# Moving the loads of q, k, v (pairs 4 to 10) and of expert 0's weights to other steps of a sorted-attention and mixture kernel

## The chip, the core and the metric

One core of a Trainium2 chip runs the whole program. A core has TensorE (PE, with its weight loads listed as PEld), VectorE (DVE), ScalarE (ACT), GpSimd (POOL), SyncE (SP) and 16 DMA engines, which all transfers share. The metric is the time of the program on the device in microseconds (us); lower is better.

## The reference

```python
for _ in range(5):                      # P: 8x8 per (batch, head)
    P = exp(P - max(P)); P /= sum(P, -1); P /= sum(P, -2)
k_sorted = einsum('bhij,bhjcd->bhicd', P, k_blocks)      # 8 blocks of 96 rows
v_sorted = einsum('bhij,bhjcd->bhicd', P, v_blocks)
scores = (q_b @ k_sorted_b.T) / 8; attn = softmax(scores)
x = (attn @ v_sorted_b) -> [3072, 512]                   # 4 batches x 768, 8 heads x 64
G = exp(x @ w_gate - max); 8 rounds: G /= rows; G /= columns; G *= 3072/8
out = sum over 8 experts e of G[:, e] * (relu(x @ w1[e]) @ w2[e])
```

The inputs are float32: q, k, v of 4 x 8 x 768 x 64, w1 of 8 x 512 x 1024, w2 of 8 x 1024 x 512.

## The kernel before, in words

The work has three parts. First, five rounds of normalisation on the 8 x 8 matrices of all 32 heads (DVE and ACT, lines 136 to 147), while the first loads run. Second, attention head by head, in 34 steps of a loop written out by hand (line 388). Third, the experts 1 to 7, which are long rows of matrix products (lines 505 to 531). Expert 0 needs x of a whole batch only, so its products are cut into pieces (`l1_piece` with w1, `l2_piece` with w2) and put between the products of the attention steps from step 9 on; `fill()` hands them out, four times a step.

Heads go in pairs: pair n holds the heads 2n and 2n + 1, and there are 16 pairs. The life of a pair is this:

- `load_pair(n)` (line 65) issues three transfers on POOL's queue, k, v and q, of 192 KB each as stored (they are cast from float32 on the way). They go to the buffers `kvr` and `qr`, of which there are six, so pair n takes the buffer of pair n - 6.
- `relayout(n)` (line 75; at step 2n - 4) is a copy on POOL from `kvr` into `kv` (two buffers). POOL works in order, so it holds up what stands behind it until k and v have landed and until the sort of pair n - 2 has read the buffer. For pair 0 ACT does it in parts.
- `build_R` (line 286) makes the sorting weights R of two heads on POOL, at each even step s for the heads s + 4 and s + 5.
- `sort_kv(g)` (line 296; at step g - 2) does six products on PE with kv and R (line 302). ACT copies their result to `kvT` (line 305; three buffers, head g takes buffer g modulo 3), and SP issues a DMA transpose of its half with v into `v1` (line 308).
- `q_transpose(n)` (line 253; at step 2n - 2) has six transposes on PE and the copies to `qT`.
- `scores(g)` (lines 317 to 324; step g), `weights(g)` (the exponential, line 328), `a_transpose(g)` (PE line 339 and an ACT copy, line 341, a step later), `attend(g)` (line 346, with `v1`), `normalise(g)`, and `x_transpose(n)` (PE line 364, ACT line 367). The heads 16 to 29 are transposed by DMA instead (line 332).

So a step's ACT work up to step 9 is the copy of line 305, the exponential, the copy of line 341, and in turn two copies of q or one of x.

The order is the program's own: `manual_schedule` keeps every engine's instructions as they are written. Each engine works in that order and waits by semaphores. Which step issues a pair's load stands in a table, `loads` (lines 385 and 386); pairs 0 to 4 are loaded ahead of everything (lines 88 to 92), pair 5 behind the first relayout (line 375), then pair 6 at step 1, 7 at 3, 8 at 5, 9 at 7, 10 at 9, 11 at 10, 12 at 11, 13 at 13, 14 at 15 and 15 at 17. `load_expert(0)` issues w1 and w2 of expert 0 (1024 KB each as stored) at the end of step 2. w1 is first used behind the gate's products at step 10, w2 at step 12.

Of the kernel before, what the change touches and what calls it, by code (L numbers as in the profile page):

```python
# [12 lines left out]
BF16 = mybir.dt.bfloat16  # L13
# [11 lines left out]
def kernel(  # L25
# [11 lines left out]
    nc = tc.nc  # L37
# [4 lines left out]
    N, Dm, E, F = 3072, 512, 8, 1024  # L42
# [22 lines left out]
    def load_pair(n):  # L65
        kv = rawp.tile([128, 2, 2, CL, D], BF16, name="kvr")
        qr = rawp.tile([128, 2, CL, D], BF16, name="qr")
        for t, r in ((k, kv[:, 0]), (v, kv[:, 1]), (q, qr)):
            nc.gpsimd.dma_start(
                out=r.rearrange("p h c d -> p h (c d)"),  # L70
                in_=bass.AP(tensor=t.tensor, offset=t.offset + 2 * n * S * D,
                            ap=[[CL * D, 128], [S * D, 2], [1, CL * D]]))
        raw_t[n] = (kv, qr)

    def relayout(n):

        kv = iop.tile([128, 2 * CL, 2, D], BF16, name="kv")
        nc.gpsimd.tensor_copy(kv.rearrange("p c t d -> p t c d"),  # L78
                              raw_t[n][0].rearrange("p t h c d -> p t (h c) d"))
        kv_t[n] = kv  # L80
# [8 lines left out]
    load_pair(1)  # L89
    load_pair(2)  # L90
    load_pair(3)
    load_pair(4)


    P9 = pp.tile([32, 9, 9], F32)
# [65 lines left out]
    wp = ctx.enter_context(tc.tile_pool(name="wp", bufs=2))  # L161
    wg = ones.tile([128, 4, E], BF16)
    w1t, w2t = [], []

    def load_expert(e):
        w1e = wp.tile([128, 4, F], BF16, name="w1e")
        w2e = wp.tile([128, 8, Dm], BF16, name="w2e")
        nc.gpsimd.dma_start(out=w1e, in_=moe_w1[e].rearrange("(kk k) f -> k kk f", k=128))  # L168
        nc.gpsimd.dma_start(out=w2e, in_=moe_w2[e].rearrange("(fb k) f -> k fb f", k=128))
        w1t.append(w1e)  # L170
        w2t.append(w2e)

    xtp = ctx.enter_context(tc.tile_pool(name="xtp", bufs=1))
    xtT = xtp.tile([128, 4, N], BF16)
# [45 lines left out]
    def batch_pieces(b):  # L220

        out_ = []
        for c in (2 * b, 2 * b + 1):
            out_ += [(0.65, l1_piece(c, fb)) for fb in range(8)]

            out_ += [(1.72, l2_piece(c, tt, nc.scalar.copy if c >= 2 and tt in (1,)
                                     else nc.vector.tensor_copy)) for tt in range(3)]
        return out_
# [9 lines left out]
    def fill():  # L238
        if slots[0] > 0:
            ahead[0] += sum(c for c, _ in pieces) / slots[0]  # L240
            slots[0] -= 1
        while pieces and ahead[0] >= pieces[0][0] / 2:
            c, run = pieces.pop(0)
            run()
            ahead[0] -= c
# [7 lines left out]
    def q_transpose(n):  # L253


        qr = raw_t[n][1]
        tq = psF.tile([128, 2, CL // 2, 128], BF16, name="psF")
        for e in range(2):
            for c in range(CL // 2):
                nc.tensor.matmul(tq[:, e, c], qr[:, e, 2 * c:2 * c + 2].rearrange("p l d -> p (l d)"),  # L260
                                 Ibf, is_transpose=True, start=True, stop=True)
        for e in range(2):
            to = qT_[0:64, n % 2, e, 0:S].rearrange(
                "p (i c l h) -> p l c i h", i=NB, l=2, h=CH)
            for l in range(2):
                (nc.vector.tensor_copy if e == 0 and n > 1 else nc.scalar.copy)(  # L266
                    to[:, l], tq[64 * l:64 * l + 64, e].rearrange("p c (i h) -> p c i h", h=CH))
# [18 lines left out]
    def build_R(eng, src, g0, n):  # L286
        eng.tensor_tensor(
            out=R[:, g0:g0 + n],
            in0=mkap(src, [src.ap[0], [1, n], [32, 8], [0, CH]], off=g0),
            in1=mkap(mask16, [mask16.ap[0], [0, n], [0, 8], [1, CH]]),  # L290
            op=ALU.mult)
# [4 lines left out]
    def sort_kv(g):  # L296

        kv, e = kv_t[g // 2], g % 2
        kvps = psB.tile([128, 2, 512], F32, name="psB")
        kvf = mkap(kvps, [kvps.ap[0], [1, CL * 128]])  # L300
        for cl in range(CL):
            nc.tensor.matmul(kvf[:, cl * 128:(cl + 1) * 128],  # L302
                             kv[:, e * CL + cl].rearrange("p t d -> p (t d)"),
                             R[:, g].rearrange("p i c -> p (i c)"), start=True, stop=True)
        nc.scalar.copy(kvT_[:, g % NKT, :, 0:96].rearrange("p i (l c) -> p i l c", c=CH),  # L305
                       mkap(kvps, [kvps.ap[0], [CH, NB], [128, CL], [1, CH]]))

        nc.sync.dma_start_transpose(
            out=v1_[:, g % NVB, :, 0:64],
            in_=kvT_[64:128, g % NKT].rearrange("p i c -> p (i c)"))  # L310

    def scores(g):

        qT, kvT = qT_[:, (g // 2) % 2, g % 2], kvT_[:, g % NKT]
        sps = psB.tile([128, 2, 512], F32, name="psB")
        for i in range(NB):
            nc.tensor.matmul(sps[:, i // 4, (i % 4) * 96:(i % 4 + 1) * 96],  # L317
                             qT[:, i * BL:i * BL + 128], kvT[:, i, 0:96],
                             start=True, stop=True)
        s4 = sps[0:96, :, 0:384].rearrange("p a (i c) -> p a i c", c=96)  # L320
        mx = sp.tile([96, 2, 4], F32, name="mx")
        nc.vector.reduce_max(out=mx, in_=s4, axis=AX.X)  # L322
        ssb = sp.tile([96, 2, 4, 96], F32, name="ssb")
        nc.vector.tensor_sub(ssb, s4, mkap(mx, [mx.ap[0], [4, 2], [1, 4], [0, 96]]))  # L324
        ssb_t[g] = ssb

    def weights(g):
        nc.scalar.activation(out=at_[:, g % NAT, :, 0:96],  # L328
                             in_=ssb_t.pop(g).rearrange("p a i c -> p (a i) c"),
                             func=AF.Exp, scale=scale)  # L330
        if g in DT:
            nc.sync.dma_start_transpose(
                out=aT_[:, g % NTT, 0:S].rearrange("p (i c) -> p i c", c=BL),
                in_=at_[:, g % NAT].rearrange("p i c -> p (i c)"))

    def a_transpose(g):
        ta = psF.tile([128, NB, 96], BF16, name="psF")
        for i in range(NB):
            nc.tensor.matmul(ta[:, i, :], at_[:, g % NAT, i], Ibf[0:96, 0:96],  # L339
                             is_transpose=True, start=True, stop=True)  # L340
        nc.scalar.copy(aT_[0:97, g % NTT, 0:S], ta[0:97].rearrange("p i c -> p (i c)"))
# [30 lines left out]
    sort_kv(0)  # L372
    build_R(nc.gpsimd, Pb, 2, 2)
    relayout(1)
    load_pair(5)
    nc.gpsimd.dma_start(out=wg, in_=moe_w_gate.rearrange("(kk k) e -> k kk e", k=128))
    NP = NH // 2
    step = {g: g + (2 if g in DT else 1) for g in range(NH)}
# [3 lines left out]
    x_step = {}  # L382
    for n in range(NP):
        x_step.setdefault(max(step[2 * n], step[2 * n + 1]) + 1, []).append(n)
    loads = {2 * n - 11: n for n in range(6, 11)}
    loads.update({10: 11, 11: 12, 13: 13, 15: 14, 17: 15})
    new = []
    for s in range(NH + 2):
        if s % 2 == 0 and s + 4 < NH:
            build_R(nc.gpsimd, Pb, s + 4, 2)  # L390
        if s < NH:
            scores(s)
        if s == 0:
            sort_kv(1)
            onesc = ones.tile([128, 128], F32)
            nc.gpsimd.memset(onesc, 1.0)
            nc.gpsimd.memset(glog[:, NT, :], EPS / 128)
            nc.gpsimd.memset(glog[:, 0:NT, E:E + 1], EPS)
        fill()
        if 0 <= s - 1 < NH and s - 1 not in DT:  # L400
            a_transpose(s - 1)
        fill()
        if s + 2 < NH:
            sort_kv(s + 2)
        if s < NH:
            weights(s)
        if s % 2 == 0:
            if 0 < s and s // 2 + 1 < NP:
                q_transpose(s // 2 + 1)
            if s // 2 + 2 < NP:  # L410
                relayout(s // 2 + 2)
        for n in x_step.get(s, []):
            x_transpose(n)
            if n % 4 == 3 and n < NP - 1:
                new = [(0.7, gate_piece(n // 4))] + batch_pieces(n // 4)
        fill()
        for g in at_step.get(s, []):
            attend(g)
            normalise(g)
        if s in loads:  # L420
            load_pair(loads[s])
        fill()
        if new:
            add(new, {9:34,17:40,26:28}[s])
            new = []
        if s == 2:
            load_expert(0)
        if s == 31:

            late_ = pp.tile([1, 8], BF16)  # L430
            nc.gpsimd.tensor_copy(late_, at_[0:1, 31 % NAT, 0, 0:8])
            load_expert(1)
# [57 lines left out]
    for it in range(8):  # L490
# [8 lines left out]
            out=gl, in0=gl, scalar=float(N) / E,  # L499
# [5 lines left out]
    for e in range(1, E):  # L505
        if e + 1 < E:
            load_expert(e + 1)
        for nc4 in range(6):
            for fb in range(AHEAD if (e, nc4) == (1, 0) else 0, 8):
                l1_tile(e, nc4, fb)  # L510
            for tt in range(4):
# [8 lines left out]
                for c0 in range(0, Dm, W):  # L520
                    oacc = psF.tile([128, Dm], F32, name="psF")
                    for fb in range(8):
# [3 lines left out]
                        out=osbl[:, t, c0:c0 + W], in0=oacc[:, 0:W],  # L526
                        scalar=glog[:, t, e:e + 1], in1=osbl[:, t, c0:c0 + W],
                        op0=ALU.mult, op1=ALU.add)
                    if e == E - 1:
                        nc.sync.dma_start(out=out[t * 128:(t + 1) * 128, c0:c0 + W],  # L530
                                          in_=osbl[:, t, c0:c0 + W])
# [30 lines left out]
```

## Time and profile before

| what | value |
|---|---|
| median of 3 runs | 761.83 us (761.48 to 763.7) |
| the profiled execution | 760.26 us, its span 758.5 us |
| mean granted TensorE clock | 0.993 |
| DMA queue of POOL (software) | 26.23 MB, 22.8% of 16 engines' span |
| DMA queue of SP (hardware) | 13.25 MB, 8.4% |
| read from HBM, written | 52.45 MB, 6.29 MB |

The profile's page gives each engine's busy time, then the span in 40 slices of 19 us with one digit of busy tenths per engine. A row of the timeline gives the start, the duration, the engine, the line, what is written and read, how often, and in brackets how long the engine sat idle before and what ended that. A row of the windows view gives the window, its length, the busy time and number of instructions of PE, PEld, DVE, ACT and POOL, the granted TensorE clock (1.00 is full speed), the share of the DMA engines and the GB/s moved. A row of the DMA view ends with the time from the issue of a transfer to its landing.

### The profile page before, as it was taken

The page shows a single profiled execution, that of the slowest core. Times are in us where ns is not written, and L with a number is a line of the kernel's source. Part 1 is how long each engine was busy: PE and PEld are TensorE (multiplying, and loading weights), DVE is VectorE, ACT ScalarE, POOL GpSimd, SP SyncE. Part 2 cuts the span into 40 slices and gives each one's busy share as a digit, 9 for nine tenths or more (in the row PEclk, how much of TensorE's full clock was granted, in tenths as well). Part 3 has the DMA queues.
Part 4 walks back from the last instruction along what each step waited for, and adds up shares of the span by engine and source line. Part 5 has one row for each costly group of instructions (what it writes and reads, how often), then busy time and mean ns, then how long its engine had stood idle before and what let it go on. Part 6 is the DMA issues. An engine that isn't in the chain of part 4 may idle for free.

```text
span 758.5 us, 10311 instructions
## 1 busy us (share of the span) xinstructions
PE 725.8 (96%) x4274; PEld 367.7 (48%) x4340; DVE 268.3 (35%) x462; ACT 331.5 (44%) x559; POOL 80.6 (11%) x105
## 2 busy tenths in 40 slices
PE   2779999999999999999999999999999999999998
PEld 2566666654444444444444444444444444444444
DVE  5788787567422122121221221212212212112122
ACT  7888887653433423324324234243242342432422
POOL 8955420000000000000000000000000000000000
PEclk9979999999999999999999999999999999999999
DMA  9999744537000600033000700051001500002112
GB/s 152 191 179 173 101 92 83 80 51 111 1 1 0 102 10 1 0 53 59 0 1 1 111 1 1 0 81 31 0 1 29 83 0 1 1 0 98 70 69 98
DMA packets 58430, 40.14 MB, mean 53 GB/s; under 512 B 30608, under 2 KB 51344, under 8 KB 58384
## 3 DMA queue, kind: packets, MB, share of 16 engines
q0 software_dynamic: 26128, 26.23, 22.8%
q1 hardware_dynamic: 32256, 13.25, 8.4%
q8 instruction: 34, 0.56, 0.3%
q14 instruction: 12, 0.10, 0.0%
HBM read 52.45 MB, written 6.29 MB: 77 GB/s over the span
## 4 chain that ended last, share of the span: by engine, by line
PE 91%; ACT 3%; DVE 3%; DMA 1%; issue 1%; ACTq 0%; DVEq 0%
PE hps L445 38%; PE psF L523 38%; PE psF L203 5%; PE psF L192 5%; DMA v__108<-kvT__106 1%; PE psB L317 1%; PE psB L302 1%; ACT kvT__106 L305 1%; PE psB L346 1%; PE psF L339 1%; DVE ssb L324 1%; ACT at__114 L328 1%; DVE mx L322 0%; ACT qT__111 L266 0%; PE psF L364 0%
## 5 line engine op out<-in xcount | busy, mean ns | idle before, releaser
L448 ACT ACTIVATE hTs<-hps 128x512 bf16<-128x512 f32 x336 | 200.6, 597 | 372.9 <-PE hps L445 365.7
L445 PE MATMUL hps<-xtT,w1e 128*128 128x512 bf16 x1317 | 295.7, 379 | 1.5
L523 PE MATMUL psF<-w2e,hTs 128*128 128x512 bf16 (+1 forms) x1325 | 295.2, 378 | 1.4
L525 DVE SCALAR_TENSOR_TENSOR osbl<-psF,glog,osbl 128x512 f32<-128x512 f32 (+1 forms) x169 | 126.3, 747 | 437.6 <-PE psF L523 425.7
L523 PEld LDWEIGHTS <-hTs 128*128 128x128 bf16 x1352 | 132.2, 98 | 157.9
L445 PEld LDWEIGHTS <-w1e 128*128 128x128 bf16 x1344 | 131.6, 98 | 158.4
L192 PE MATMUL psF<-xtT,w1e 128*128 128x384 bf16 x256 | 49.0, 326 | 0.6 <-ACT qT__111 L266 0.6
L168 POOL DMA_DIRECT2D w1e<-in_moe_w_dram x8 | 6.1, 768 | 394.3 <-PE hps L445 370.4
L203 PE MATMUL psF<-w2e,hTs 128*128 128x512 bf16 x180 | 44.2, 379 | 0.6
L195 ACT ACTIVATE hTs<-psF 128x384 bf16<-128x384 f32 x64 | 29.7, 499 | 7.4 <-PE psF L192 6.8
L322 DVE TENSOR_REDUCE mx<-psB 96x8 f32<-96x768 f32 x32 | 30.4, 949 | 5.8 <-PE psB L317 5.4
L324 DVE TENSOR_TENSOR ssb<-psB,mx 96x768 f32<-96x768 f32 x32 | 30.5, 954 | 3.2
L305 ACT CAST kvT__106<-psB 128x768 bf16<-128x768 f32 x32 | 25.9, 809 | 11.6 <-issue 7.1
L192 PEld LDWEIGHTS <-w1e 128*128 128x128 bf16 x256 | 22.9, 98 | 12.7 <-issue 1.0
L328 ACT ACTIVATE at__114<-ssb 96x768 bf16<-96x768 f32 x32 | 27.3, 854 | 1.8 <-DVE ssb L324 1.8
L203 PEld LDWEIGHTS <-hTs 128*128 128x128 bf16 x192 | 17.8, 100 | 17.0
L78 POOL COPY kv<-kvr 128x1536 bf16<-128x1536 bf16 x15 | 22.0, 1468 | 30.5 <-issue 16.6
L355 DVE TENSOR_TENSOR og__236<-psB,den 96x512 bf16<-96x512 f32 x32 | 22.0, 686 | 1.1
L346 PE MATMUL psB<-v__108,aT__115 97*128 97x65 bf16 x256 | 13.6, 199 | 7.4 <-ACT kvT__106 L305 5.2
L302 PE MATMUL psB<-R,kv 128*128 128x128 bf16 x192 | 18.6, 242 | 1.9 <-ACT kvT__106 L305 0.9
L260 PE MATMUL psF<-Ibf,qr 128*128 128x128 bf16 x96 | 9.7, 248 | 11.0 <-DMA qr<-in_q_dram 11.0
L317 PE MATMUL psB<-kvT__106,qT__111 128*128 128x96 bf16 x256 | 18.0, 219 | 2.2 <-ACT kvT__106 L305 1.5
(82 smaller groups left out, 275.1 us busy)
## 6 DMA issues: line engine op xcount, KB each, us to landing
w1e<-in_moe_w_dram POOLq DMA_DIRECT2D x8, 1024.0 KB, 8.0
w2e<-in_moe_w_dram POOLq DMA_DIRECT2D x8, 1024.0 KB, 8.7
out_dram<-osbl SPq DMA_DIRECT2D x23, 256.0 KB, 2.0
kvr<-in_k_dram POOLq DMA_DIRECT2D x16, 192.0 KB, 7.6
kvr<-in_v_dram POOLq DMA_DIRECT2D x16, 192.0 KB, 7.6
qr<-in_q_dram POOLq DMA_DIRECT2D x16, 192.0 KB, 7.6
v__108<-kvT__106 SPq DMA_TRANSPOSE x32, 4.6
out_dram<-osbl SPq DMA_DIRECT2D x2, 128.0 KB, 1.7
```

What stands on the lines that cost most here:

```text
L192: nc.tensor.matmul(hps[:, 0:HC], w1t[0][:, kk, fb * 128:(fb + 1) * 128], xtT[:, kk, c * HC:(c + 1) * HC], start=(kk == 0), stop=(kk == 3))
L195: nc.scalar.activation(out=hT0[c][:, fb, 0:HC], in_=hps[:, 0:HC], func=AF.Relu)
L203: nc.tensor.matmul(oacc, hT0[c][:, fb, tt * 128:(tt + 1) * 128], w2t[0][:, fb, :], start=(fb == 0), stop=(fb == 7))
L302: nc.tensor.matmul(kvf[:, cl * 128:(cl + 1) * 128], kv[:, e * CL + cl].rearrange("p t d -> p (t d)"), R[:, g].rearrange("p i c -> p (i c)" ...
L305: nc.scalar.copy(kvT_[:, g % NKT, :, 0:96].rearrange("p i (l c) -> p i l c", c=CH), mkap(kvps, [kvps.ap[0], [CH, NB], [128, CL], [1, CH]]))
L322: nc.vector.reduce_max(out=mx, in_=s4, axis=AX.X)
L324: nc.vector.tensor_sub(ssb, s4, mkap(mx, [mx.ap[0], [4, 2], [1, 4], [0, 96]]))
L328: nc.scalar.activation(out=at_[:, g % NAT, :, 0:96], in_=ssb_t.pop(g).rearrange("p a i c -> p (a i) c"), func=AF.Exp, scale=scale)
L445: nc.tensor.matmul(hps, w1t[e][:, kk, fb * 128:(fb + 1) * 128], xtT[:, kk, nc4 * 512:(nc4 + 1) * 512], start=(kk == 0), stop=(kk == 3))
L448: nc.scalar.activation(out=hT[e, nc4][:, fb, :], in_=hps, func=AF.Relu)
L523: nc.tensor.matmul(oacc[:, 0:W], hT[e, nc4][:, fb, tt * 128:(tt + 1) * 128], w2t[e][:, fb, c0:c0 + W], start=(fb == 0), stop=(fb == 7))
L525: nc.vector.scalar_tensor_tensor(out=osbl[:, t, c0:c0 + W], in0=oacc[:, 0:W], scalar=glog[:, t, e:e + 1], in1=osbl[:, t, c0:c0 + W], op0=A ...
```

## The change

Pair 4 is no longer loaded at the start but at step 2, pair 5 at step 4, pair 6 at step 6, pairs 7 and 8 at steps 7 and 8, pairs 9 and 10 at step 9; from pair 11 on the steps stay. The weights of expert 0 are loaded apart: w1 at the end of step 1, w2 at the end of step 7. Nothing else changes.

```diff
     load_pair(3)
-    load_pair(4)
...
+    def load_w1(e):
+        w1t.append(wp.tile([128, 4, F], BF16, name="w1e"))
+        nc.gpsimd.dma_start(out=w1t[e], in_=moe_w1[e].rearrange("(kk k) f -> k kk f", k=128))
+
+    def load_w2(e):
+        w2t.append(wp.tile([128, 8, Dm], BF16, name="w2e"))
+        nc.gpsimd.dma_start(out=w2t[e], in_=moe_w2[e].rearrange("(fb k) f -> k fb f", k=128))
+
     def load_expert(e):
...
+        load_w1(e)
+        load_w2(e)
...
     relayout(1)
-    load_pair(5)
...
-    loads = {2 * n - 11: n for n in range(6, 11)}
-    loads.update({10: 11, 11: 12, 13: 13, 15: 14, 17: 15})
+    loads = {2: [4], 4: [5], 6: [6], 7: [7], 8: [8], 9: [9, 10], 10: [11], 11: [12], 13: [13], 15: [14], 17: [15]}
...
-        if s in loads:
-            load_pair(loads[s])
+        for n in loads.get(s, ()):
+            load_pair(n)
         fill()
...
-        if s == 2:
-            load_expert(0)
+        if s == 1:
+            load_w1(0)
+        if s == 7:
+            load_w2(0)
```

POOL's order in the new kernel, from the end of the rounds on, is: R, relayout(1), gate weights, R, relayout(2), w1, R, relayout(3), pair 4, R, relayout(4), pair 5, R, relayout(5), pair 6, pair 7, w2, R, relayout(6), pairs 8, 9 and 10, R, relayout(7), pairs 11 and 12, R, relayout(8), pair 13, and on as before.

More of the change, by code (lines that the diff above doesn't have):

```diff
@@ L163 @@
     w1t, w2t = [], []
-    def load_expert(e):
[L166 to L171, printed above, removed]
+    def load_w1(e):
[4 more added lines that the diff above has]
+        nc.gpsimd.dma_start(out=w2t[e], in_=moe_w2[e].rearrange("(fb k) f -> k fb f", k=128))
+    def load_expert(e):
+        load_w1(e)
+        load_w2(e)
     xtp = ctx.enter_context(tc.tile_pool(name="xtp", bufs=1))
```

## The prediction

> **What bounds the kernel now.** I read the page's shares first, then its slices, then the trace around the stretch that the change touches.
>
> ```profile
> PE 725.8 (96%) x4274; PEld 367.7 (48%) x4340; DVE 268.3 (35%) x462; ACT 331.5 (44%) x559; POOL 80.6 (11%) x105
> ...
> ACT  7888887653433423324324234243242342432422
> ...
> DMA  9999744537000600033000700051001500002112
> ```
>
> PE is the bound of the whole, but not from the start: in the first two or three slices of 19 us ACT is busy at 8 tenths and the DMA engines at 9. The steps 0 to 9 lie there (the scores of line 317 of step 3 begin at 26.63 us, of step 5 at 32.96, of step 9 at 48.19, of step 10 at 51.41). From step 10 on the pieces of expert 0 fill PE, and the order of PE's work is the same in both kernels. So what the change can give or take it gives before 51.4 us, and what it may break later is a wait of PE's, which costs its full length.
>
> Next, what ACT waited for between 31 and 52 us, in the timeline:
>
> ```profile
> 31.94 0.80 ACT L305 CAST kvT__106<-psB 128x768 bf16<-128x768 f32 x1
> ...
> 35.97 0.80 ACT L305 CAST kvT__106<-psB 128x768 bf16<-128x768 f32 x1 [0.80 <-DMA v__108<-kvT__106]
> ...
> 39.45 0.80 ACT L305 CAST kvT__106<-psB 128x768 bf16<-128x768 f32 x1 [0.17 <-DMA v__108<-kvT__106]
> ...
> 43.52 0.80 ACT L305 CAST kvT__106<-psB 128x768 bf16<-128x768 f32 x1 [0.54 <-DMA v__108<-kvT__106]
> ...
> 47.03 0.80 ACT L305 CAST kvT__106<-psB 128x768 bf16<-128x768 f32 x1
> ...
> 50.30 0.80 ACT L305 CAST kvT__106<-psB 128x768 bf16<-128x768 f32 x1
> ```
>
> Line 305 runs once a step and writes one of three buffers, so it must wait until the transpose of three heads before has been read out. Three times it waited for that DMA: 0.80 + 0.17 + 0.54 = 1.51 us. The chain of waits has the longest of these transposes as one piece:
>
> ```profile
> 32.77 10.65 DMA v__108<-kvT__106
> 43.52 0.81 ACT kvT__106 L305
> ```
>
> Why so slow? The DMA view of the stretch from 26 to 29 us gives issue to landing:
>
> ```profile
> w1e<-in_moe_w_dram POOLq DMA_DIRECT2D x1, 1024.0 KB, 9.5
> w2e<-in_moe_w_dram POOLq DMA_DIRECT2D x1, 1024.0 KB, 16.1
> ...
> v__108<-kvT__106 SPq DMA_TRANSPOSE x1, 9.7
> ```
>
> The transpose issued at 26.20 took 9.7 us, the one at 29.30 10.0, the one at 32.77 10.6; the one at 23.05, before the weights, took 5.5, and at 77.70, with little else moving, 3.8. The weights of expert 0, issued at 25.99 and 26.80 and landed at 35.5 and 42.9, are what they shared the engines with.
>
> Last, the clock and PE's gap, from the windows view and PE's timeline:
>
> ```profile
> 27.20:37.44 10.24, 6.21 (x116) 5.26 (x113) 8.62 (x14) 8.90 (x15) 9.62 (x12) 1.00 1.19 191
> 37.44:47.68 10.24, 8.64 (x97) 7.76 (x94) 8.39 (x14) 8.29 (x13) 3.84 (x5) 0.50 1.30 178
> 47.68:57.92 10.24, 7.88 (x135) 6.43 (x136) 8.58 (x17) 8.63 (x15) 7.99 (x11) 1.00 1.33 181
> ```
> ```profile
> 36.82 0.40 PE L346 MATMUL psB<-v__108,aT__115 97*128 97x65 bf16 x8 [1.70 <-ACT kvT__106 L305]
> ```
>
> The granted clock (third column from the end) was 0.50 from 37.44 to 47.68, right behind PE's gap of 1.70 us, which is ACT's wait for the transpose handed on. In that stretch ACT's line 341 waited 0.28 + 0.34 + 0.60 us for PE's line 339.
>
> **The change part by part.** PE, ACT, DVE and SP keep their order; only POOL's changes. No instruction is added or removed.
>
> *Early steps (pairs 4 and 5 and w2 later, w1 from step 2 to 1).* POOL has 0.72 us for each of six issues less to do before its relayout at step 0 (20.39 us now); by the rows that leaves w1 issued at 20.1 us, when the queue holds only the small gate weights, as pairs 0 to 3 have landed by 17.6. At 8.0 us to landing (the page's median for w1) it lands at 28.1; at 9.5, at 29.6. Pair 4 follows behind it: issued from 23.6 (after step 1's sort, whose product ends at 22.1, and a relayout of 1.48), its v lands two transfers behind w1. A transfer of 192 KB takes 1.36 us in a full queue (w2 landed at 42.9, the sixth behind it at 51.0) and 1.2 us around 22 us; so 30.8, and relayout(4) is done at 32.3. It is needed by the sort of step 6, now at 38.33, some 37.5 then: 5 us of cover.
>
> *The gain.* The transposes of steps 3 to 7, which now share with w1 and w2, then share with one pair at a time, and land in 4 to 6 us (the 3.8 and 5.5 above) where about 9 is the slack. So the 1.51 us of direct waits go. What is late next is ACT itself: from 47.03 to 50.30 a step took 3.27 us with ACT idle for none of it, and from 28.48 to 31.94 it took 3.46 with waits for DVE. The five steps from 31.94 to 50.30 took 18.36 us; five of 3.27 are 16.35, three of 3.27 and two of 3.46 are 16.73. That is a gain of 1.63 to 2.01 if the clock stays up, and 1.51 if it still falls and PE's share of the waits stays. I take 1.8: between 47.68 and 51.09 PE was busy for 2.11 of 3.41 us at full clock and the clock held, between 34.03 and 37.44 for 1.51 and it fell; the steps freed of the gap come nearer to the first.
>
> [...]
>
> *Pairs 5 to 7, each behind the one before.* POOL works in order: relayout(n) waits for pair n, and pair n+1 is issued only behind it. Unloaded, k lands 3.5 us and v 4.6 us after its issue (at 77.81 and 78.57). So pair 5 goes out at 32.3, its v lands at 37.6, relayout(5) ends at 39.1 (needed at step 8, about 44); pair 6 goes out at 39.1, k lands at 42.6, v at 44.4; relayout(6) ends at 46 (needed at step 10, about 52). Each has 5 us of cover. These cost nothing, but the DMA engines idle for some 4 us between them, and what is left comes late and together: pairs 7 to 12 and w2.
>
> *The new queue at steps 7 to 10.* POOL lets eight transfers be open, as the trace shows:
>
> ```profile
> 36.31 0.76 POOL L69 DMA_DIRECT2D kvr<-in_k_dram  x1
> 43.14 0.71 POOL L69 DMA_DIRECT2D kvr<-in_v_dram  x1 [6.06 <-DMA w2e<-in_moe_w_dram]
> 44.53 0.71 POOL L69 DMA_DIRECT2D qr<-in_q_dram  x1 [0.68 <-DMA kvr<-in_k_dram]
> ```
>
> v of pair 9 waited for w2, issued eight before it, and q for k of pair 7. In the new order the one eight behind w2 is v of pair 10, and queued behind that on POOL stand R for step 10 (line 287, 0.66 us) and relayout(7) (1.46), which the sort of step 12 needs. Call w2's landing W. v goes out at W + 0.3, q waits for k of pair 8 (W + 1.36) and ends at W + 2.4, R ends at W + 3.0, relayout(7) at W + 4.5. That sort now runs at 62.57, so 60.8 with 1.8 gained: free if W is before 56.3. From k of pair 6 at 42.6, five transfers of 1.2 to 1.36 and w2 at 7.4 (35.5 to 42.9) give W = 56.0 to 57.2, so a wait of 0 to 0.9; with transfers of 1.0 (landings at 9.7, 10.8, 11.7 at the start) and 6.5 (29.0 to 35.5) W = 54.1. I take 0.3. w2's first use (63.5 now) has 5 us left. The same for relayout(8), ready at about W + 12.3 for a sort at some 69: less pressed.
>
> Transposes of steps 7 to 10 now meet the backlog instead; between 43 and 60 us they took 8.2 to 8.5 beside pairs alone, inside the slack. I cost that at nothing; without cover it is the 0.2 to 0.8 a step of the rows above. w1 is used first at 53.85 and is 20 us early.
>
> *Sum.* 1.8 - 0.3 = 1.5 us. The profiled execution took 760.26 us (span 758.5): 758.8. The median of the runs shown is 761.83, 1.57 above it; on that I put the forecast, **760.3 us**. 0.3%, about what a measurement of this kernel can tell from no change, is 2.3 us: the whole stretch is hardly longer in waits than that.
>
> **The rivals.**
> - *POOL's queue becomes the wait (the slower side).* Place: POOL, v of pair 10 behind w2, and PE's sort of step 12 behind relayout(7). Point: W later than 56.3 costs its excess, later than 58.1 eats the whole 1.8. For it: w2 needed 16.1 us from issue to landing in this trace with w1's rest ahead of it; issued at 43.4 with five transfers ahead, 16.1 gives W = 59.5, a wait of 3.2 and a net loss of 1.4: 763.2. Against: most of those 16.1 us were w1's.
> - *The transposes stay slow.* If it was the weights' traffic that starved them, w1 now sits before the transposes of 23.05 and 26.20, and backlog comes back at step 7. Then only part of the 1.51 goes: 0.5 gained, 761.3. For it: of the two transposes beside w1 alone the second took 9.7. Against: they are needed at 31.9 and 35.1, 9 us after issue, and from 28.1 only a pair shares with them. [...]
> - *More is gained.* All DMA waits, all PE waits of ACT (2.73 us idle by the rows: 0.80, 0.28, 0.17, 0.34, 0.54, 0.60) go and nothing comes back: 2.7, so 759.1.
>
> **How the numbers follow.** Forecast (gain of 1 to 2.2) 50%; POOL's queue 20%; transposes still slow 12%; more gained 18%. The range, 758.2 to 762.9, reaches from a little past the last to most of the first. Over 2.3 us faster: the last and a bit of the forecast's upper end, 24%. Over 2.3 slower needs W past 60.4: 10%. Within 0.3%: 66%.
>
> **What would show it.** Right: line 305 no longer waits for the transposes at steps 5 to 7; transposes issued at 29 to 40 us land in under 7 us; no stretch at clock 0.50 behind 37 us; scores of step 10 begin at about 49.6. POOL's line 69 waits for w2 at about 50 to 56 us, and line 302 of step 12 starts at once or up to 1 us late. Wrong: that line waits for POOL's line 78 by more than 2 us, at step 12 or at 6, 8 or 10 (a pair that lands later than 5 us); or the clock falls in spite of the filled gap; or the profile of another execution has the slow clock elsewhere, which would move the base itself by about 1 us.

## The result

The changed kernel takes 764.71 us (median of 15 runs, 762.87 to 768.79), the kernel before 761.66 (15 runs, 760.1 to 763.7). The ratio is 1.0046, with an interval of 1.0031 to 1.0062. So the change makes the kernel slower by about 0.5%, where the forecast was 0.2% faster, and the time lies above the range.

The profiled execution took 764.71 us, its span is 762.9. I set it beside the profiled execution of before (760.26, span 758.5) by the start of each step's scores (line 317 before, line 320 after):

| step | before, us | after, us | after minus before |
|---|---|---|---|
| 0 | 15.91 | 16.30 | 0.39 |
| 3 | 26.63 | 27.02 | 0.39 |
| 4 | 29.76 | 32.23 | 2.47 |
| 10 | 51.41 | 52.56 | 1.15 |
| 11 | 56.72 | 60.77 | 4.05 |
| 18 | 86.28 | 90.19 | 3.91 |
| 19 | 89.88 | 94.30 | 4.42 |
| 31 | 139.2 | 143.6 | 4.4 |

Step 3 loses 2.1 us. Steps 4 to 9 win back 1.3 (20.33 us where before took 21.65). Step 10 loses 2.9 (8.21 against 5.31), step 18 another 0.5. After that the two run alike.

### The profile page after: what moved, and what is told of

The parts are those of the page before. It is cut to its first block, busy times and chain, and to the rows that moved or that the text cites. A ratio compares the mean times of both kernels' runs of the same rounds, so it can differ in the third digit from the quotient of the medians.

```text
span 762.9 us, 10382 instructions
## 1 busy us (share of the span) xinstructions
PE 732.9 (96%) x4340; PEld 370.5 (49%) x4340; DVE 268.4 (35%) x462; ACT 332.4 (44%) x559; POOL 80.6 (11%) x105
## 4 chain that ended last, share of the span: by engine, by line
PE 91%; DMA 3%; ACT 3%; DVE 1%; issue 1%; POOL 1%; ACTq 0%; DVEq 0%; POOLq 0%
PE psF L528 38%; PE hps L450 38%; PE psF L206 5%; PE psF L195 5%; DMA v__103<-kvT__101 1%; PE psB L320 1%; PE psB L305 1%; PE psB L349 1%; DMA qr<-in_q_dram 1%; ACT kvT__101 L308 1%; DMA aT__110<-at__109 1%; PE psF L342 1%; ACT qT__106 L269 1%; DVE ssb L327 1%; ACT at__109 L331 0%
## 5 line engine op out<-in xcount | busy, mean ns | idle before, releaser
L195 PE MATMUL psF<-xtT,w1e 128*128 128x384 bf16 x256 | 50.9, 334 | 0.6 <-ACT qT__106 L269 0.6
L308 ACT CAST kvT__101<-psB 128x768 bf16<-128x768 f32 x32 | 25.8, 806 | 12.6 <-issue 6.0
```

The source lines that it names most:

```text
L195: nc.tensor.matmul(hps[:, 0:HC], w1t[0][:, kk, fb * 128:(fb + 1) * 128], xtT[:, kk, c * HC:(c + 1) * HC], start=(kk == 0), stop=(kk == 3))
```

## The profile after

The page of the changed kernel, shares and slices:

```profile
PE 732.9 (96%) x4340; PEld 370.5 (49%) x4340; DVE 268.4 (35%) x462; ACT 332.4 (44%) x559; POOL 80.6 (11%) x105
...
ACT  7787887744342332423424324233243342332422
...
DMA  9999944455100420015000600042001500002112
```

The sums say little. PE is busy 7.1 us longer by the page, but the trace of before has 4274 of the 4340 products and this one all of them, so part of that is missing records. The DMA row says more. Its fifth slice (76 to 95 us) is 9 where it was 7: the loads end later. The last load of a pair lands at 92.17 us, at 85.20 before.

**Step 3.** ACT's timeline, line 308 (305 before):

```profile
31.14 0.80 ACT L308 CAST kvT__101<-psB 128x768 bf16<-128x768 f32 x1 [1.81 <-DMA v__103<-kvT__101]
...
34.43 0.80 ACT L308 CAST kvT__101<-psB 128x768 bf16<-128x768 f32 x1 [0.30 <-DMA v__103<-kvT__101]
```

The waits for the transposes are gone at steps 5 to 7, as predicted, and there is a longer one at step 3. PE's timeline shows it handed on:

```profile
31.99 0.40 PE L349 MATMUL psB<-v__103,aT__110 97*128 97x65 bf16 x8 [2.22 <-ACT kvT__101 L308]
```

The chain of waits names what was late, and the DMA view from 20 to 24 us shows it beside w1:

```profile
23.44 10.90 DMA v__103<-kvT__101
```
```profile
w1e<-in_moe_w_dram POOLq DMA_DIRECT2D x1, 1024.0 KB, 10.4
v__103<-kvT__101 SPq DMA_TRANSPOSE x2, 10.8
```

w1 was issued at 20.06 and landed at 30.50, after 10.4 us. The transposes issued at 20.29 and 23.44 took 10.7 and 10.9; those issued at 16.28 and 18.60, with no pair 4 or 5 in the queue, took 2.8 and 2.5. The one of 20.29 is read out at 31.04, and the copy that must wait for it would have begun 1.8 us sooner.

**The clock.** The windows view, with the granted clock in the third column from the end:

```profile
29.96:33.37 3.41, 1.26 (x24) 1.06 (x24) 1.04 (x4) 2.23 (x4) 0.00 (x0) 1.00 1.61 157
33.37:43.61 10.24, 8.88 (x104) 8.29 (x105) 8.92 (x16) 8.97 (x13) 5.76 (x7) 0.50 0.89 112
43.61:53.85 10.24, 6.24 (x117) 5.30 (x114) 9.37 (x16) 9.48 (x15) 10.22 (x14) 1.00 1.14 153
53.85:60.68 6.83, 6.56 (x61) 4.70 (x62) 3.27 (x7) 4.38 (x8) 1.94 (x3) 0.50 1.25 184
```

It falls behind PE's gap of step 3 (2.22 us, ending at 31.99), as before it fell behind one of 1.70, and again at 53.85. This second fall lies in step 10, where expert 0's pieces begin and PE is the bound: PE is busy 6.56 of 6.83 us there at half speed. That is the 2.9 us of step 10. No gap as long as that of step 3 stands ahead of it (0.80 us, and one of 1.01 within which it falls), but in the 3.41 us ahead of it PE was busy for only 1.68:

```profile
50.44:53.85 3.41, 1.68 (x34) 1.52 (x33) 3.05 (x6) 3.10 (x5) 3.41 (x6) 1.00 1.31 192
```

**POOL's queue.** POOL's timeline (the row of a load is its issue):

```profile
24.05 0.76 POOL L69 DMA_DIRECT2D kvr<-in_k_dram  x1
...
34.41 1.46 POOL L78 COPY kv<-kvr 128x1536 bf16<-128x1536 bf16 x1 [7.50 <-PE psB L305]
35.82 0.76 POOL L69 DMA_DIRECT2D kvr<-in_k_dram  x1
...
42.10 1.46 POOL L78 COPY kv<-kvr 128x1536 bf16<-128x1536 bf16 x1 [3.42 <-PE psF L263]
43.51 0.76 POOL L69 DMA_DIRECT2D kvr<-in_k_dram  x1
...
47.83 0.90 POOL L170 DMA_DIRECT2D w2e<-in_moe_w_dram  x1
...
61.95 0.72 POOL L69 DMA_DIRECT2D kvr<-in_v_dram  x1 [5.86 <-DMA w2e<-in_moe_w_dram]
```

Pair 4 goes out at 24.05 behind w1; its v lands at 34.26. relayout(4), at 34.41, waited 7.50 us for that. (The row names PE's line 305, but the sort that frees the buffer, at step 3, began at 28.29. The releaser shown is only what ended last; the landing is the one that fits.) Pair 5 goes out at 35.82, and relayout(5) waits for its landing at 41.95. So pair 6 is issued at 43.51 and w2 at 47.83, and w2 lands at 61.66.

## The experiments

Three theories were weighed, under letters or words that the expectations give. One is that w1's packets make the transposes of steps 0 and 1 late, and that this is the loss (P): in the kernel before, from 30 to 34 us beside w1, POOL's queue moved 331 packets and SP's 332 (DMA view), and a transpose has 544 (SP's count from 77.6 to 81.8 us, with one alone). One is that the loads on POOL's queue come late, and that what they hold up is the loss (Q). One is that PE's gaps cost half speed (0.50 was granted behind gaps of 1.70 us before and 2.22 after), and that the clock is the loss. Each expectation was written before its run. Ratios are to the kernel before, run beside it. e4, e5 and e15 have four or five runs each, the others eight to twelve. The times of e4, e10 and e16 came out as expected; so did e11's, by luck, since its transposes did not get faster. The others came out by another case of the expectation or outside it.

| kernel | base | median us | ratio | interval |
|---|---|---|---|---|
| after | - | 764.71 | 1.0046 | 1.0031 to 1.0062 |
| e1_half_rows | after | 763.83 | 1.0039 | 1.0019 to 1.0058 |
| e2_half_parts | after | 765.52 | 1.0049 | 1.0035 to 1.0064 |
| e3_weights_only | before | 761.22 | 0.9999 | 0.9986 to 1.0012 |
| e4_pairs_only | after | 765.97 | 1.0064 | 1.0042 to 1.0086 |
| e5_unread_after | after | 765.81 | 1.0065 | 1.0042 to 1.0087 |
| e6_unread_before | before | 761.36 | 1.0000 | 0.9988 to 1.0012 |
| e7_parts_p10 | e2 | 763.56 | 1.0019 | 1.0009 to 1.0030 |
| e8_parts_p10_unread | e7 | 765.17 | 1.0036 | 1.0025 to 1.0048 |
| e9_w2_step4 | e2 | 763.0 | 1.0021 | 1.0009 to 1.0033 |
| e10_dt20 | e8 | 762.71 | 1.0024 | 1.0005 to 1.0043 |
| e11_before_parts | before | 761.01 | 0.9997 | 0.9987 to 1.0008 |
| e12_before_spread | before | 762.02 | 1.0009 | 0.9997 to 1.0020 |
| e13_pairs45_early | after | 760.78 | 0.9987 | 0.9979 to 0.9996 |
| e14_two_ahead | after | 763.2 | 1.0018 | 1.0007 to 1.0028 |
| e15_w2_step4_unread | e9 | 764.8 | 1.0039 | 1.0026 to 1.0053 |
| e16_before_half_rows | before | 760.18 | 0.9983 | 0.9972 to 0.9993 |
| e17_early_half_rows | e13 | 761.35 | 0.9998 | 0.9983 to 1.0012 |
| e18_early_half_rows_unread | e17 | 760.93 | 0.9987 | 0.9976 to 0.9999 |

### w1 in two transfers: e1 and e2

e1 loads w1 of expert 0 as two halves of each row (packets of 1 KB, not 2 KB: 0.31 MB in 305 packets of POOL's queue from 19 to 24 us). e2, the control, loads two halves of the rows (packets stay 2 KB: 0.36 MB in 174).

```diff
...                                          # for e = 0 alone
+        for f0 in range(0, F, F // 2):       # e1
+            nc.gpsimd.dma_start(out=w1t[e][:, :, f0:f0 + F // 2],
+                                in_=moe_w1[e][:, f0:f0 + F // 2].rearrange("(kk k) f -> k kk f", k=128))
+        for k0 in range(0, 4, 2):            # e2
+            nc.gpsimd.dma_start(out=w1t[e][:, k0:k0 + 2],
+                                in_=moe_w1[e][k0 * 128:(k0 + 2) * 128].rearrange("(kk k) f -> k kk f", k=128))
```

> The changed kernel, but w1 of expert 0 goes as two transfers, each of half of every row, so that a packet carries 1 KB as stored and not 2 KB. Theory P (the DMA engines take turns between POOL's queue and the transposes packet by packet, so a transpose of 544 packets waits for as many packets of w1, and their length sets its time): the transposes issued at 20.3 and 23.4 us land in 6 to 8 us and not 10.8, line 308's wait of 1.81 us at step 3 goes, the scores of step 4 begin 1.5 to 2 us earlier (30.3 to 30.7), and the time falls by 1 to 2 us against the changed kernel, to 762.7 to 763.7. Theory B (the bytes queued ahead set it): nothing changes, 10.8 us and 764.7. Theory C (the whole loss is the clock's fall at 53.85 us): the step-3 wait may go, but the time follows only the clock.

> The control for the run with half rows: also two transfers for w1, but each of half of the row blocks, so that packets keep 2 KB. Theory P: as the changed kernel, transposes of 20.3 and 23.4 us take 10 to 11 us, step 3 waits 1.8 us, 764.7. If it was the size of one transfer and not of its packets that held the transposes, this one helps as much as the half rows, 762.7 to 763.7.

In both, the transposes of steps 0 and 1 took 6.3 and 8.6 us, and the wait of step 3 was gone: the scores of step 4 began at 29.73 (e1) and 29.85, those of step 10 at 49.35 and 49.63, 2.06 and 1.78 us ahead of before. So the packets' length was not what told here; two transfers of whole rows did as much. And the kernel was no better for it. PE's timeline of e1, then PE's waits of e2:

```profile
63.24 0.51 PE L310 MATMUL psB<-R,kv 128*128 128x128 bf16 x6 [1.41 <-POOL kv L78]
```
```profile
PE psB L310 <- POOL kv L78: 3.6, 1, 3.6
```

The sort of step 12 (line 310 here) waits for relayout(7), which stands behind v of pair 10 and w2. That is the rival of the prediction, and the late step 3 and the slow step 10 of the changed kernel had covered it. In e2 the clock fell in this wait as well (0.50 from 65.38 to 68.79), and step 12 took 9.16 us in place of 4.05. e1's ten times spread from 761.82 to 766.83 and its profiled run (762.19) is one of the low ones, so what its other runs waited for is not seen.

### Each half of the change alone: e3 and e4

e3 keeps the pairs as before and moves only the weights; e4 moves only the pairs.

```diff
+    load_pair(4)                             # e3, against after
+    load_pair(5)
-    loads = {2: [4], 4: [5], 6: [6], 7: [7], 8: [8], 9: [9, 10], ...
+    loads = {1: [6], 3: [7], 5: [8], 7: [9], 9: [10], ...
-        if s == 1:                           # e4, against after
-            load_w1(0)
-        if s == 7:
-            load_w2(0)
+        if s == 2:
+            load_expert(0)
```

> The kernel before with the weights alone moved (w1 at step 1, w2 at step 7; pairs as before). w1 then stands behind pairs 5 and 6 and moves at about 29 to 35.5 us, as in the kernel before. Theory P: the transposes issued at 26.2 and 29.3 us are held to about 36, so the first wait at step 5 (0.8 us) stays, those of steps 6 and 7 behind w2 go; 0.5 to 1 us faster than before, 760.7 to 761.2. If moving w2 is itself what cost the time (its packets then beside steps 9 to 12), this kernel is slower than before by 2 us or more.

> The changed kernel's pair loads with both weights at step 2, behind pair 4. Pair 5 is then issued at about 31 us behind w1 and w2 and lands at about 45, its relayout ends at 47, and the sort of step 8 (about 46) waits for it by 1 to 2 us; pair 6 is issued at 47 and its relayout ends at about 53, in time for step 10. Theory P: slower than before by 2 to 4 us, 764 to 766. If the pairs' lateness costs nothing and only w1's place did, it is as before, 761.7.

The weights alone change nothing that can be measured; the pairs alone cost 0.64%. The waits of e4 from 22 to 80 us:

```profile
POOL kv L78 <- DMA kvr<-in_v_dram: 15.8, 2, 14.4
...
PE psB L349 <- ACT kvT__101 L308: 7.6, 7, 3.1
...
PE psB L305 <- POOL kv L78: 2.4, 1, 2.4
```

Pair 5, issued at 30.95 behind w1 and w2, held a relayout for 14.4 us, and a sort waited 2.4. So the cost is in moving the pairs. But e4's waits are not those of the changed kernel, which has w1 ahead of pair 4 and no weights between pairs 4 and 5.

### The clock: e5 and e6

Both add to steps 3 to 10 eight products that nobody reads, to keep PE busy; nothing is left out.

```diff
+        if 3 <= s <= 10:
+            unread = psF.tile([128, 512], F32, name="psF")
+            for _ in range(8):
+                nc.tensor.matmul(unread[:, 0:128], Ibf, Ibf, start=True, stop=True)
```

> The changed kernel with eight unread products of 128 columns on PE ahead of attend at each of the steps 3 to 10, into a bank that nobody reads; they fill the gaps in which PE waits for ACT. If the clock's fall (33 to 44 and 54 to 61 us) is the whole loss, the time goes back to the kernel before or below, 761.5 or less. If the clock is one of three terms: the granted clock stays at 1.00 from about 30 us on and step 10 takes 5.3 us and not 8.2, but step 3 still waits 1.8 us for the transpose, and POOL's queue behind w2 now shows: line 305 of step 12 waits 1 to 3 us for relayout(7) (line 78), which the slow step 10 had covered. Then 763 to 764.5.

> The kernel before with the same unread products. The clock stays at 1.00 from 27 us on; the three waits of ACT for the transposes stay (1.5 us). Gain 0.3 to 0.8 us, 760.5 to 761, and a narrower spread of the runs. If the clock cost the kernel before as much as the changed one, 2 us or more.

In e5 the clock still fell behind step 3, for 3.41 us in place of 10.24, and stood from there through step 10 (windows view). Step 10 took 5.75 us in place of 8.21, and the gain went at once into another wait of PE's, at step 12 (waits view), behind which the clock fell again, from 67.14 to 70.55:

```profile
36.40:67.10 30.70, 23.82 (x392) 19.55 (x391) 24.03 (x40) 26.16 (x43) 20.76 (x27) 1.00 1.14 159
```
```profile
PE psB L305 <- POOL kv L78: 2.4, 1, 2.4
```

In e6 the mean clock was 1.000 (0.993 before) and the time the same. The half clock is real and lies where the time is lost in the profile, but to take it out of step 10 wins nothing: the queue stands right behind it. The runs without a profile say the same. Their mean granted clocks are on record, and in the 15 runs of the changed kernel the time does not follow them: 763.8 us at 0.984, 765.94 at 0.998, and the three longest (767.68 to 768.79) have 0.988 and 0.989, as has the profiled run of 764.71.

### Patching the late waits one by one: e7 to e10, e15

e7 is e2 with pair 10 loaded a step later, behind relayout(7). e8 is e7 with the unread products. e9 is e2 with w2 at step 4. e15 is e9 with the unread products. e10 is e8, with attention's transposes made by DMA from head 20 on in place of 16.

```diff
-    loads = {2: [4], 4: [5], 6: [6], 7: [7], 8: [8], 9: [9, 10], 10: [11], ...
+    loads = {2: [4], 4: [5], 6: [6], 7: [7], 8: [8], 9: [9], 10: [10, 11], ...   # e7, e8, e10
-        if s == 7:
+        if s == 4:                                                              # e9, e15
             load_w2(0)
-    DT = range(16, NH - 2)
+    DT = range(20, NH - 2)                                                      # e10
```

> The kernel with w1 in two parts of e2, with pair 10 loaded at step 10 behind relayout(7) and not at step 9 ahead of it, so that POOL meets the eighth transfer behind w2 after relayout(7). If POOL's queue behind w2 is what cost e1 and e2 their gain: the wait of PE's sort of step 12 for line 78 goes (1.4 us in e1, about 5 in e2), and the time falls to 761 to 762 (the clock may still fall near step 10). If that wait only moves to the sort of step 14 (relayout(8) behind pairs 10, 11 and 12), 763 to 765.

> e7 with the unread products of e5. With all three terms taken away (transposes held by w1, the clock, POOL's queue) what the change was forecast to gain should be left: the scores of step 10 at 49.3 to 49.8 us, step 10 at 5.3 us, and 758.5 to 760. If a fourth cost is at work, it stays at 761 or more.

> The changed kernel with w1 in two parts (as e2) and w2 at the end of step 4, behind pair 5, where the changed kernel leaves the DMA engines idle, and not at step 7. Theory Q (the loads need the DMA engines nearly all the time to about 76 us; the change lets them idle for some 8 us around steps 4 to 7, so the queue ends that much later, and first POOL's relayout(7) and then the first heads transposed by DMA wait for it): the queue ends some 7 us earlier than in e7, no wait of line 305 for line 78 at step 12 and none of attend for the DMA transpose at step 18; 760 to 761.5, at least as fast as the kernel before. If w2's traffic costs wherever it lies, ACT's waits for the transposes come back at steps 5 to 8 and it stays at 762.5 or more.

> e8 with the DMA transposes of the exponentials beginning at head 20 and not at head 16; heads 16 to 19 are transposed on PE. In e8 PE waited 3.4 us at step 18 for the transpose of head 16 (issued at 83.5, landed 9.3 us later, behind the last pairs). Theory Q: that wait goes, PE gets 4 x 0.34 us of products more and ACT four copies of 0.8; net 1 to 2.5 us faster than e8, 762.7 to 764.2. If the wait at step 18 only stands in for something later (ACT, the relayout of pair 9), no change, 765.

> e9 (w1 in two parts, w2 at step 4) with the unread products of e5 at steps 3 to 10. In e9 the clock was at 0.50 from 50 to 56.8 us, step 10 took 7.5 us and the scores of step 11 began 1.2 us later than in the kernel before, though those of step 9 began 1.7 earlier. If the clock is what eats e9's lead: step 10 takes 5.3, step 11 begins 1.3 to 1.8 us earlier than before, and 760 to 761. If the late queue takes the lead in its place: line 305 waits for line 78 by 1 to 2.5 us at step 12 and attend for the transpose at step 18, and it stays at 762 to 763.5.

e7: the wait of step 12 went, and there came 0.5 at step 14 and 2.1 at step 18, where head 16's attention is the first to be transposed by DMA. e8 waited longer there. Its unread products did not hold the clock in step 10 (0.50 from 51.84 to 55.25; the step took 7.39 us, 6.96 in e7), nor did they in e10. PE's timeline of e8, then PE's waits of e10:

```profile
92.83 0.62 PE L354 MATMUL psB<-v__103,aT__110 97*128 97x65 bf16 x8 [3.40 <-DMA aT__110<-at__109]
```
```profile
PE psB L310 <- POOL kv L78: 1.9, 1, 1.9
```

That transpose was issued at 83.52 and took 9.26 us, with the queue of pairs still running (the last pair landed at 90.6). With it put off to head 20 (e10) the median fell by 2.5 us from e8, as I expected, but the intervals of the two ratios overlap, and 1.9 us of wait stood at step 14 now. e9 brought w2 in at 49.4 in place of 60.27 and missed its forecast: waits of 0.6 at step 10 (for relayout(6), since pair 6 now went behind w2) and 1.0 at step 18, and a clock of 0.50 from 50.0 to 56.8 (step 10 took 7.51 us). In e15 the clock fell all the same, from 50.4 to 57.3, and ACT waited 1.2 us for a transpose; so it does not tell how much of e9 was the clock. Every patch showed the next late transfer: the last load of a pair landed between 88.9 and 92.5 in these five, at 85.20 in the kernel before.

### Pairs 4 and 5 alone: e13, and everything earlier: e14

e13 puts only pairs 4 and 5 back to the start. e14 keeps the new order and loads the pairs 4 to 9 one to four steps earlier, most of them two or three.

```diff
+    load_pair(4)                             # e13
+    load_pair(5)
-    loads = {2: [4], 4: [5], 6: [6], 7: [7], ...
+    loads = {6: [6], 7: [7], ...                                        # e13
+    loads = {0: [4], 1: [5], 2: [6], 4: [7], 6: [8], 8: [9], 9: [10], ...  # e14
```

> The changed kernel with pairs 4 and 5 loaded at the start as before; pairs 6 to 10 and the weights as changed. Theory Q (idle DMA engines early, a late queue afterwards): the transfers still stop between w1 (landed about 31) and pair 6 (issued about 37 to 39), so w2 lands at 55 to 58 and the queue still ends late; 762.5 to 764.5. If it was the lateness of pairs 4 and 5 (their relayouts held behind w1) that cost the time, it is as the kernel before, 761.5.

> The changed kernel's order of loads, but each pair two steps earlier: pair 4 at step 0, 5 at 1, 6 at 2, 7 at 4, 8 at 6, 9 at 8, 10 at 9; w1 at step 1, w2 at step 7. Theory Q: the transfers follow each other without a stop, the queue ends at about 76 us as in the kernel before, no wait for line 78 at steps 12 or 14, none for the DMA transposes at step 18; 760.5 to 762 (ACT's waits beside w1 stay, 0.5 to 1.5 us). If step order as such costs the time, 763 or more.

e13 is faster than the changed kernel, and by 0.13% than the kernel before: 0.9987 (0.9979 to 0.9996), with every run below 761.4. I had expected it to lose still, by the queue. POOL's timeline of e13:

```profile
28.47 1.47 POOL L78 COPY kv<-kvr 128x1536 bf16<-128x1536 bf16 x1 [3.20 <-issue]
...
34.92 1.46 POOL L78 COPY kv<-kvr 128x1536 bf16<-128x1536 bf16 x1 [4.38 <-issue]
36.33 0.76 POOL L69 DMA_DIRECT2D kvr<-in_k_dram  x1
...
40.64 0.94 POOL L171 DMA_DIRECT2D w2e<-in_moe_w_dram  x1
...
57.84 0.71 POOL L69 DMA_DIRECT2D kvr<-in_v_dram  x1 [6.88 <-DMA w2e<-in_moe_w_dram]
60.53 1.46 POOL L78 COPY kv<-kvr 128x1536 bf16<-128x1536 bf16 x1
```

relayout(4) runs at 28.47 (34.41 in the changed kernel), pair 6 goes out at 36.33 (43.51), w2 at 40.64 (47.83); what is issued behind relayout(4) goes some 7 us earlier, and w2 lands at 57.55 (61.66). w1 is issued 1.7 us later, at 21.78, since pair 5's three issues stand ahead of relayout(2) again. The transposes of 19.89 and 23.04 take 5.4 and 8.7 us, and ACT's line waits for none: the one of 23.04 lands at 31.74, the copy that needs it starts at 31.93. Step 10 starts at 49.39, 2.0 us ahead of before; steps 4 to 9 took 19.64 us. Of this, step 10 (6.79 us, clock 0.50 for 3.41) and a wait of 1.1 us at step 18 give some back.

e14 had neither the wait for line 78 nor that of step 18, but w1 went out only at 23.96, behind two pairs, and the transposes beside it took 12.4 and 11.8 us. ACT's waits:

```profile
ACT kvT__101 L308 <- DMA v__103<-kvT__101: 3.4, 2, 2.9
```

So with a timely queue the transposes cost 2.9 us at one place, and with timely transposes (e2) the queue costs 3.6. Both theories hold a part of the loss; e13 mends both at once.

### The transposes in the kernel before: e11, e12, e16

e11 loads w1 and w2 in two parts of whole rows each, at step 2; e12 the same four parts at steps 2 to 5; e16 loads w1 in half rows, as e1 does, and w2 as before.

```diff
+                nc.gpsimd.dma_start(out=w1e[:, k0:k0 + 2], ...     # e11: k0 = 0, 2; w2e likewise
+        if s in (2, 3, 4, 5):                                      # e12
+            load_part(s - 2)
+                nc.gpsimd.dma_start(out=w1e[:, :, f0:f0 + F // 2], ...  # e16: f0 = 0, F // 2
```

> The kernel before with w1 and w2 of expert 0 each in two parts, all four at step 2. In e2 a transpose beside w1 in parts took 6.3 and 8.6 us, and beside the whole w1 10.7 and 10.9. If the boundary between two transfers lets the transposes through, those issued at 26.2 to 36.8 us land in 6 to 8.5 us and not 9.5 to 10.6, ACT's 1.5 us of waits shrink to under 0.5, and the time falls by 0.5 to 1.5 us, to 760.2 to 761.2. If it was w1's place, and not its parts, that helped in e2, no change: 761.6.

> The kernel before with w1 and w2 in four parts, one at the end of each of the steps 2 to 5, pairs as before. The queue stays full but a pair's short packets stand between the parts. Theory Q and the parts together: transposes of steps 1 to 7 in 6 to 8.5 us, no wait of ACT over 0.3 us, queue's end as before, 760 to 761. If parts do nothing, 761.6; if the parts' issues (0.75 us each) delay POOL's relayouts, PE's line 302 waits for line 78 and it is slower than before.

> The kernel before with w1 as two transfers of half rows, packets of 1 KB as w2's, where e11 kept 2 KB. Theory P (the engines take turns packet by packet, and the length of the other queue's packets sets a transpose's time): transposes issued at 26 to 33 us land in 8 to 9 us and not 10 to 11, ACT's waits of 0.80, 0.17 and 0.54 fall to under 0.5 in all, and the time by 0.5 to 1.5 us, 760 to 761. If the length does nothing, as e11: 761 to 761.6.

e11: the transposes took 11.4 to 11.8 us (9.7 to 10.6 before), ACT waited 2.4, and the time was the same. e12: 9 to 11, 1.7, the same. e16: the transposes of 26.19 and 29.30 took 7.0 and 8.1 in place of 9.7 and 10.0. ACT's waits of e16 for them are

```profile
ACT kvT__106 L310 <- DMA v__108<-kvT__106: 0.4, 1, 0.4
```

in place of 1.51 us, step 10 begins at 50.0 in place of 51.41, and the time is 760.18, 0.9983 (0.9972 to 0.9993): the lowest median here. It leaves the order of the loads alone.

### Both together: e17 and e18

e17 is e13 with w1 in half rows, e18 is that with the unread products.

> e13 (pairs 4 and 5 at the start, the rest as changed) with w1 in two transfers of half rows as e16, the two that were each faster than the kernel before (0.9987 and 0.9983). If their gains come from the same ACT waits behind w1 they do not add: 760.0 to 760.8. If half rows save more (the transposes beside w1 took 8.7 and 6.9 us in e13, with no ACT wait left), 759.5 or less.

> e17 with the unread products of e5 at steps 3 to 10. In e13 the clock was at 0.50 from 51.2 to 54.6 us and step 10 took 6.8 us against 5.3. If the clock is all that was lost there: 1 to 1.5 us faster than e17, 758.5 to 759.5. If, as in e5, POOL's queue behind w2 takes its place (line 306 of step 12 waits for line 78 by 1 to 1.5 us), no change against e17; the unread products may also cost up to 0.5.

The gains do not add. e17's step 10 took 5.3 us at full clock (0.998 is the mean of the profiled run), but the attention of step 18 then waited 1.9 us for its DMA transpose, and e18, with a mean clock of 0.999, waited 2.3 there.

## Why the prediction was wrong, step by step

- **w1 "lands at 28.1; at 9.5, at 29.6".** It took 10.4 us and landed at 30.50. The sum went on with the first of the two, the page's median over eight experts; expert 0's own row of 9.5 was the nearer one. The issue came at 20.06 where 20.1 was forecast, by luck: only pair 5's three issues stood behind POOL's wait for the rounds, not six, and in e1, e2 and e5 w1 went out at 19.64 to 19.68; the changed kernel's profile is 0.39 us late there.
- **"so 30.8, and relayout(4) is done at 32.3", with "5 us of cover".** This step failed. v of pair 4 landed at 34.26, relayout(4) was done at 35.9; 2.4 of the 3.5 us are w1's. Its own sort was not delayed; but the relayout holds POOL, and I weighed the cover against the sort and not against what POOL issues behind it. The prediction let pair 5 go out at 32.3 and pair 6 at 39.1; they went at 35.82 and 43.51. e13 shows the price of this step and the next together: with pairs 4 and 5 back the ratio goes from 1.0046 to 0.9987, which is the whole loss and a gain besides.
- **The transposes "are needed at 31.9 and 35.1, 9 us after issue".** This step failed too, and it is where most of the difference from e13 arises (step 10 begins at 52.56 against 49.39). The transposes of 23.05 and 26.20 were priced; the one issued at 20.29, which the earlier w1 now meets as well, was left out. It took 10.7 us, and line 308 of step 3 was 1.8 us late for it. Only one row of a transpose beside w1 (9.7 us) stood against that slack, and it had not had w1's whole passage beside it. The rival of the slow transposes (12%) named this starving, but priced it as a smaller gain, 761.3, and not as a new wait.
- **"W = 56.0 to 57.2", "54.1".** w2 landed at 61.66. The term that was mis-sized is the issue, 47.83 where some 43.4 was reckoned: 4.4 us late, by the step above. From issue to landing it took 13.8, and the sum had 12.6 to 13.4 (its 57.2 is a slip: five transfers of 1.36 and 7.4 on 42.6 give 56.8).
- **The rival of POOL's queue** (20%) named the right place: v of pair 10 waited 5.86 us for w2. In the changed kernel the sort of step 12 did not wait, because PE was late itself by then; in e1, e2 and e5 it waited 1.41, 3.6 and 2.4.
- **The gain of 1.8** was about right as a mechanism: steps 4 to 9 took 2.0 us less than before in e1 and e13, 1.3 in the changed kernel, with half a clock.
- **The clock.** "no stretch at clock 0.50 behind 37 us" failed: 0.50 until 43.61 and from 53.85 to 60.68. The prediction saw the clock only as a term of the gain, behind a gap; in the profiled run it fell a second time behind a stretch with little work for PE (busy for 1.68 of 3.41 us), at step 10, where it costs 2.9 us. e5 shows that without this fall the kernel is no faster, and e6 that the kernel before gains nothing by a full clock.
- **Transposes of steps 7 to 10 at nothing**: right, no wait for them (7.0 to 9.2 us). What was not looked at is step 18, where the queue's late end (92.17) meets head 16's transpose (issued at 87.19, 6.2 us, 0.5 us lost; 1.1 to 3.4 in e13, e7 and e8).

What stays open: how the half clock lies over the steps in the runs without a profile; why parts of whole rows relieve the transposes in e2 and not in e11, where w2 follows directly; and why e17 is not faster than e13. The 0.39 us that the changed kernel's profile is late already at step 0 are not the change's: q of pair 1 landed at 12.40 (11.73 before), and PE's transposes of it stand ahead of PE's work on the result of the rounds; in e5, with the same loads up to there, it landed at 11.57 and step 0 began at 15.92.

## What to carry to other kernels

When a load is moved closer to its use, do not ask only whether it lands before its reader: a copy that waits for it on an in-order engine holds every load issued behind it, so the lateness passes on to transfers that were never touched (7 us here, met again at steps 12, 14 and 18). A large transfer that is moved earlier meets other small transfers than before; list each one that now lies beside it, with its own due time. And one stall may stand in front of another: the gain of mending it is known only when the one behind it has been measured too.

## What the runs showed of the hardware

In two stretches beside a large load the transposes moved packet for packet with the load. The DMA view from 23 to 28 us of the changed kernel, beside w1, and from 35 to 38 us of before, beside w2:

```profile
q0 software_dynamic: 440, 0.90, 94.8%
q1 hardware_dynamic: 440, 0.11, 17.1%
```
```profile
q0 software_dynamic: 462, 0.47, 92.0%
q1 hardware_dynamic: 460, 0.12, 29.5%
```

POOL's queue (q0) and SP's (q1) moved the same number of packets: 440 and 440 in 5 us with packets of 2 KB (0.90 MB by 440), 462 and 460 in 3 us with packets of 1 KB (0.47 MB by 462). So in these stretches a packet of the transpose went for each packet of the load: 88 a us beside w1, 153 beside w2. That fits what half rows did: in e16, from 28 to 33 us, SP's queue moved 544 packets beside 706 of POOL's (0.70 MB), where before it moved 360 beside 483 (0.85 MB), and the transpose beside w1 took 7.0 us in place of 9.7. So the pace rose, though not one to one. It does not explain e2, where whole rows let the transposes through in 6.3 and 8.6 us, nor e11, where they took 11.4 to 11.8 beside whole rows.

The other thing I had not expected is where the clock falls. Between 30 and 110 us it stood at 0.50 once in the kernel before, for 10.24 us, and twice in the changed kernel, for 10.24 and 6.83. The length of PE's gap does not tell these falls from the rest: ahead of them it was 1.70 us in the kernel before and 2.22 in the changed kernel, but at the second fall 0.80 and 1.01, and gaps of 0.80 and 1.00 ahead of 51.15 and 52.98 in the kernel before were followed by none. PE's busy time in 3.41 us does. The windows view of before, ahead of its fall and behind it:

```profile
34.03:37.44 3.41, 1.51 (x31) 1.40 (x30) 2.18 (x4) 2.58 (x5) 2.79 (x3) 1.00 1.23 191
...
47.68:51.09 3.41, 2.11 (x38) 1.80 (x39) 3.23 (x7) 3.32 (x6) 3.41 (x5) 1.00 1.29 193
```

PE was busy for 1.51 us ahead of this fall, and for 1.26 and 1.68 ahead of the two of the changed kernel. From 47.68 to 51.09 of before it was busy for 2.11, from 43.61 to 47.02 of the changed kernel for 2.24 and from 47.02 to 50.44 for 2.32, and the clock stayed at 1.00 behind each. Whether PE's busy time is the cause was not shown.
